# An uneven layout of w_down: 13 rows on the lower 64 partitions, 11 on the upper 64

## The chip, the cores and the metric

One core of one Trainium2 chip (trn2). The metric is the device time of one execution in microseconds; lower is better. "Span" is the time from the first to the last instruction in the profile, about 1.3 us less than the device time. In this document the lower engines are the DMA engines 0 to 7, and the upper ones 8 to 15.

## The reference, cut to what matters

One decode step of a transformer block, batch 2, width 640: a modulated layernorm, attention over a cache (32 heads, head size 192, the last 1024 positions), then a second modulated layernorm and a gated feed-forward layer with F = 1536.

```python
h = _layernorm(x) * (1 + ca) + sa
x = x + ga * _A_ref(h, A_k_cache, A_v_cache, A_wq, A_wo)
h = _layernorm(x) * (1 + cb) + sb
x = x + gb * (_gelu(h @ w_gate) * (h @ w_up) @ w_down)     # w_down: 1536 x 640, bf16
```

The kernel reads 76.88 MB, of which w_down is 1.97 MB. w_down is the last thing to be loaded.

## The kernel before

All large tensors are loaded by SyncE, in one fixed order, into one large SBUF tensor ("arena"), each load as soon as its space is free. Partition p of w_down holds rows 12p to 12p+11, so each partition has 12 rows of 1280 bytes. Four loads bring them: rows 9 to 11, 0 to 4, 5 to 7, 8.

```python
    WO_SPLIT = [(0, 28), (28, 17), (45, 3)]
    WD_SPLIT = [(9, 3), (0, 5), (5, 3), (8, 1)]
    ...
            if kind == "wd":
                r0, nr = WD_SPLIT[it[1]]
                return B_w_down.rearrange("(p r) n -> p (r n)", r=FC)[:, r0 * D:(r0 + nr) * D]
    ...
        def pump(*consumed):             # issues every load whose space is free
            ...
                queue["ops"][it] = S.dma("sp", k_dma(view(it), source(it)), sem_of[it], writes=keys(it), ...)
    ...
        # a = gelu(gate) * up, transposed to one column per row of w_down
        S.op("dve", lambda e: e.tensor_copy(out=aT[:, :, 0:RM:RB], in_=ps[:, 2, 0:FC * B]...), name="aT")
        for ci, (r0, nr) in enumerate(WD_SPLIT):
            def f(e, r0=r0, nr=nr):
                for fc in range(r0, r0 + nr):
                    wv = wd_v[:, fc, :].rearrange("p (i n) -> p i n", i=NR)
                    for i in range(NR):
                        last = e.matmul(ps[32 * i:32 * i + RM, BK_OT, CY:CY + DR], lhsT=aT[:, fc, :], rhs=wv[:, i, :], ...)
                return last
            S.op("pe", f, reads=["aT"] + keys(("wd", ci)), writes=[bank(BK_OT)], name="down%d" % ci)
        # then two VectorE operations (times gb, plus x) and the store
```

## Time and profile before

| | before |
|---|---|
| median, six runs | 186.31 us (186.21 to 186.68) |
| span of the profiled run | 185.0 us |
| DMA share of the chain that ended last | 57% |
| mean rate of the DMA engines | 416 GB/s |

The page's list of DMA queues. Its columns are packets, megabytes, and the time of those packets as a share of sixteen engines' span.

```profile
q1 hardware_dynamic: 3180, 76.88, 97.2%
q8 instruction: 5, 0.08, 0.2%
q10 hardware_dynamic: 16, 0.01, 0.0%
q14 instruction: 1, 0.01, 0.0%
```

The engines are busy with the kernel's own loads for 97% of the span.

The end of the chain of waits: start, duration, what.

```profile
155.23 26.50 DMA arena<-in_B_w_down_dram
181.73 0.04 issue
181.77 0.74 PE ps L690 x16
182.51 0.02 issue
182.54 0.34 DVE fin L695
182.87 0.02 issue
182.89 0.33 DVE finb L697
```

The down matmuls (L690) in the timeline: start, duration, engine, line, operation, operands, and in brackets how long the engine had been idle and what ended that.

```profile
179.88 0.39 PE L690 MATMUL ps<-arena,aT 128*17 128x160 bf16 x12 [0.30 <-DVE aT L682]
180.62 0.53 PE L690 MATMUL ps<-arena,aT 128*17 128x160 bf16 x20 [0.36 <-DMA arena<-in_B_w_down_dram]
181.77 0.71 PE L690 MATMUL ps<-arena,aT 128*17 128x160 bf16 x16 [0.62 <-DMA arena<-in_B_w_down_dram]
```

A load over 128 partitions is done when all sixteen engines have reported. The trace records each report. Here are two of the loads, their sixteen landings in order, in us from the start (worked out of the landing records, not a view of the profile):

```
first w_down load (rows 9-11): 176.66 .71 .75 .76 .80 .83 .96 177.08 .23 .39 .47 .77 | 178.33 .51 .60 .67
last w_down load (row 8):      180.23 .27 .28 .31 .38 .51 .62 .75 .94 .98 181.29 | 181.84 .90 182.03 .09 .12
```

All sixteen have the same bytes to move, yet four, and at the end five, are late. The five packets of the queue "instruction" start at 36.96, 96.64, 133.22, 160.87 and 178.05 us; each packet takes 0.99 to 1.08 us, and after each of them one more landing of every later load is late. (The 8 KB packet of queue 14, at 89.43 us, sets one engine back in the same way, by 1.0 us; that engine is not among the five, but is the next latest.) The Trainium skill, "Runtime: NRT & Kernel Launch", section "Instruction fetch mechanics", says that an engine's instruction memory is refilled in 16 KiB blocks, fetched by a DMA queue that the sequencer drives itself. The trace agrees: five packets of 16384 bytes, of the kind "instruction". The kernel's loads never pause, and no late engine caught up again before the end.

### The profile page before, as it was taken

The page shows a single profiled execution, that of the slowest core. Times are in us where ns is not written, and L with a number is a line of the kernel's source. Part 1 is how long each engine was busy: PE and PEld are TensorE (multiplying, and loading weights), DVE is VectorE, ACT ScalarE, POOL GpSimd, SP SyncE. Part 2 cuts the span into 40 slices and gives each one's busy share as a digit, 9 for nine tenths or more (in the row PEclk, how much of TensorE's full clock was granted, in tenths as well). Part 3 has the DMA queues.
Part 4 walks back from the last instruction along what each step waited for, and adds up shares of the span by engine and source line. Part 5 has one row for each costly group of instructions (what it writes and reads, how often), then busy time and mean ns, then how long its engine had stood idle before and what let it go on. Part 6 is the DMA issues. An engine that isn't in the chain of part 4 may idle for free.

```text
span 185.0 us, 1611 instructions
## 1 busy us (share of the span) xinstructions
PE 107.2 (58%) x835; PEld 28.5 (15%) x558; DVE 106.7 (58%) x99; ACT 14.5 (8%) x27; POOL 6.5 (4%) x27
## 2 busy tenths in 40 slices
PE   0015720857766379662499565966662499715472
PEld 0011100040000000001252000600001266401231
DVE  6213000119699488965991999789975938202411
ACT  2032100140000000001000000010001000101610
POOL 7600000000000000000000000000000000000000
PEclk9999995555799966998559999999999569996576
DMA  9989999999898989999998989899999999999990
GB/s 324 449 376 436 462 446 404 434 425 494 377 489 361 510 361 489 436 414 457 395 461 383 478 383 489 383 468 436 418 446 404 442 403 449 398 414 426 406 383 34
DMA packets 3202, 76.97 MB, mean 416 GB/s; under 512 B 378, under 2 KB 508, under 8 KB 1148
## 3 DMA queue, kind: packets, MB, share of 16 engines
q1 hardware_dynamic: 3180, 76.88, 97.2%
q8 instruction: 5, 0.08, 0.2%
q10 hardware_dynamic: 16, 0.01, 0.0%
q14 instruction: 1, 0.01, 0.0%
HBM read 76.88 MB, written 0.00 MB: 416 GB/s over the span
## 4 chain that ended last, share of the span: by engine, by line
DMA 57%; DVE 24%; PE 16%; ACT 1%; issue 1%; SPq 1%
DMA arena<-in_A_k_cache_dram 35%; DMA arena<-in_B_w_down_dram 14%; DVE arena L504 14%; PE ps L567 9%; DMA arena<-in_w_mod_dram 8%; DVE S_sb L523 6%; PE ps L516 3%; DVE Em L553 2%; PE ps L456 2%; DVE negm L533 1%; ACT E_sb L541 1%; SPq L283 1%; PE ps L544 1%; PE ps L537 1%; DVE M L529 0%
## 5 line engine op out<-in xcount | busy, mean ns | idle before, releaser
L516 PE MATMUL ps<-arena,ident_b 128*128 128x512 bf16 x192 | 51.3, 412 | 25.8 <-DVE arena L504 25.8
L504 DVE TENSOR_TENSOR arena<-arena,qbc 128x3072 bf16<-128x3072 bf16 x32 | 54.8, 1750 | 8.3 <-DMA arena<-in_A_k_cache_dram 8.3
L567 PE MATMUL ps<-arena,Em 128*64 128x384 bf16 x256 | 26.6, 379 | 5.7 <-DVE Em L553 5.7
L523 DVE TENSOR_REDUCE S_sb<-ps 128x32 f32<-128x1024 f32 x16 | 19.5, 1218 | 10.1 <-PE ps L516 10.1
L567 PEld LDWEIGHTS ps<-arena,Em 128*64 128x64 bf16 x256 | 16.4, 128 | 31.0 <-DVE Em L553 22.2
L553 DVE TENSOR_TENSOR Em<-E_sb,maskE 128x2048 bf16<-128x2048 bf16 x8 | 18.0, 2283 | 3.4 <-PE ps L567 3.4
L478 PE MATMUL ps<-arena,hT 128*2 128x512 bf16 x60 | 6.7, 625 | 9.1 <-DMA arena<-in_A_wq_dram 8.1
L531 PEld LDWEIGHTS ps<-ident_f,M 128*1 128x1 f32 x2 | 0.2, 80 | 60.5 <-DVE M L529 60.5
L488 DVE CAST qrow<-ps 128x512 bf16<-128x512 f32 x1 | 0.7, 692 | 15.0 <-PE ps L478 15.0
L627 PE MATMUL ps<-arena,oT 128*2 128x512 bf16 (+1 forms) x96 | 4.0, 312 | 4.7 <-DMA arena<-in_A_wo_dram 4.7
L635 DVE COPY arena<-ps 128x128 f32<-128x128 f32 x1 | 0.3, 292 | 10.5 <-PE ps L627 10.5
L541 ACT ACTIVATE E_sb<-S_sb,nbias 128x256 bf16<-128x256 f32 x2 | 1.0, 508 | 65.8 <-DVE nbias L539 65.8
L574 ACT ACTIVATE On<-ps,rden 128x384 bf16<-128x384 f32 x2 | 1.2, 580 | 49.5 <-PE ps L567 49.5
L397 PE MATMUL ps<-ident_b,crow 2*128 2x2 bf16 x5 | 0.4, 177 | 7.9 <-DMA crow<-in_c_dram 7.9
L456 PE MATMUL ps<-arena,scT 128*17 128x480 bf16 x40 | 4.3, 597 | 0.7 <-DMA arena<-in_w_mod_dram 0.7
L410 PE MATMUL ps<-st,selstat 128*128 128x2 f32 x4 | 1.1, 348 | 6.1 <-ACT sqj L406 6.1
L402 DVE CAST X<-xr 128x160 f32<-128x160 bf16 x1 | 0.2, 245 | 6.4 <-DMA xr<-in_A_x_dram 6.4
L661 PE MATMUL ps<-arena,h2T 128*2 128x384 bf16 x40 | 3.6, 507 | 0.3 <-DVE h2T L441 0.3
L494 PE MATMUL ps<-qrow,selq 128*128 128x192 bf16 x16 | 2.7, 361 | 1.2 <-ACT qrow L485 1.2
L464 DVE TENSOR_SCALAR opc<-modR 128x160 f32<-128x160 f32 x2 | 0.5, 244 | 4.7 <-ACT modR L461 4.7
L437 PE MATMUL ps<-selrow,hrow 128*32 128x2 bf16 x40 | 0.7, 182 | 3.6 <-DVE hrow L428 3.6
L478 PEld LDWEIGHTS ps<-arena,hT 128*2 128x2 bf16 x20 | 0.6, 107 | 14.3 <-DMA arena<-in_A_wq_dram 9.9
(84 smaller groups left out, 52.8 us busy)
## 6 DMA issues: line engine op xcount, KB each, us to landing
arena<-in_A_v_cache_dram SPq DMA_DIRECT2D x4, 6144.0 KB, 25.8
arena<-in_A_k_cache_dram SPq DMA_DIRECT2D x3, 6144.0 KB, 39.2
arena<-in_A_k_cache_dram SPq DMA_DIRECT2D x2, 3072.0 KB, 42.5
arena<-in_w_mod_dram SPq DMA_DIRECT2D x1, 4800.0 KB, 14.2
arena<-in_A_wq_dram SPq DMA_DIRECT2D x1, 4608.0 KB, 31.2
arena<-in_A_wo_dram SPq DMA_DIRECT2D x1, 4480.0 KB, 25.8
arena<-in_A_wq_dram SPq DMA_DIRECT2D x1, 3072.0 KB, 20.7
arena<-in_A_wo_dram SPq DMA_DIRECT2D x1, 2720.0 KB, 31.9
```

The costliest lines, as they stand in the source:

```text
L283: return lambda e: e.dma_start(dst, src)
L456: last = e.matmul(ps[32 * i:32 * i + RM, half, 0:MH].rearrange("p (m n) -> p m n", n=DR), lhsT=scT[:, k, :], rhs=wv[:, 3 * half:3 * half + ...
L478: last = e.matmul(ps[32 * i:32 * i + B, n, :], lhsT=hT[:, k, :], rhs=wv[:, kk, i, n * QW:(n + 1) * QW], start=(k == 0), stop=(k == KT - 1) ...
L494: last = e.matmul(ps[:, BK_T + b, 0:Dh], lhsT=selq[:, b, u * P:(u + 1) * P], rhs=qrow[:, u * Dh:(u + 1) * Dh], start=(u == 0), stop=(u == ...
L504: S.op("dve", lambda e: e.tensor_tensor(out=kt, in0=kt, in1=qbc[:, b, :].unsqueeze(1).broadcast_to([P, JC, Dh]), op=ALU.mult), reads=[("qb ...
L516: last = e.matmul(o_ap, lhsT=ident_b[:, :], rhs=kt[:, :, t * GC:(t + 1) * GC], start=(t == 0), stop=(t == NCH - 1))
L523: S.op("dve", lambda e: e.tensor_reduce(out=S_sb[:, b, 2 * JC * pair:2 * JC * (pair + 1)], in_=ps[:, 2 * z:2 * z + 2, :].rearrange("p k (j ...
L541: S.op("act", lambda e: e.activation(out=E_sb[:, b, :], in_=S_sb[:, b, :], func=ACTF.Exp, scale=SCALE, bias=nbias[:, b:b + 1], accum_out=d ...
L553: S.op("dve", lambda e, z=z, j=j: e.tensor_tensor(out=Em[:, z, :, :], in0=E_sb[:, b, j:j + JE].unsqueeze(2).broadcast_to([P, JE, H]), in1= ...
L567: last = e.matmul(ps[64 * i:64 * i + 2 * H, BK_O, 0:ON], lhsT=Em[:, z, 2 * jp:2 * jp + 2, :].rearrange("p j h -> p (j h)"), rhs=view(it, l ...
L627: last = e.matmul(ps[32 * i:32 * i + B, bk, 0:w], lhsT=oT[:, t, :], rhs=wv[:, tl, lo:lo + w], start=(t < NR), stop=(t >= NT - NR), tile_po ...
L661: last = e.matmul(ps[32 * i:32 * i + B, bk, 0:FT].rearrange("p (m r) -> p m r", r=FR), lhsT=h2T[:, k, :], rhs=wk[:, i, :, :], start=(k == ...
```

## The change

Its intent, as I read it: if the engines that end last are upper ones, let them carry less of the last tensor. Row 11 of each upper partition moves to the lower partition 64 below it. The Trainium skill, "DMA: Bandwidth & Descriptors", sections "The descriptor swizzle" and "Why a DMA increments its semaphore by 16 and not by 1", says that a load over 128 partitions gives partitions 0 to 63 to engines 0 to 7 and the others to 8 to 15, and that a load whose slowest dimension is 8 runs on the eight lowest engines only. So eight loads of eight partitions each bring both rows to the lower half. The upper half's two slots are zeroed by GpSimd, so whatever activations they meet have no effect; one more transpose matmul makes the thirteenth column of activations.

```diff
-    WD_SPLIT = [(9, 3), (0, 5), (5, 3), (8, 1)]
+    WD_SPLIT = [(9, 2), (FC - 1, 2), (0, 5), (5, 3), (8, 1)]
+    HALF = P // 2
+    XA, XB, XC = 8, 4, 2
...
+        def load_half(it):
+            z = view(it)
+            S.op("pool", lambda e: e.memset(z, 0.0), writes=keys(it), name="half0")
+            src = B_w_down.rearrange("(p r) n -> p r n", r=FC)[:, FC - 1, :].rearrange("(s c a b) n -> c b a s n", s=2, c=XC, a=XA)
+            for n in range(XB * XC):
+                c, b = divmod(n, XB)
+                p0 = c * XA * XB + b
+                S.dma("sp", k_dma(z[p0:(c + 1) * XA * XB:XB, :].rearrange("p (s n) -> p s n", s=2), src[c, b]), sem_of[it],
+                      writes=half_key(n) if n else keys(it), name="ld_half%d" % n)
...
+            c0 = 2 * FC
+            last = e.matmul(ps[0:HALF, 2, c0:c0 + B], lhsT=aR[:, :].rearrange("p (m r) -> p m r", r=FR)[:, HALF:P, FR - 1], rhs=selg[:, NR - 1, :],
+                            start=True, stop=True)
```

(Cut: the larger views, the thirteenth column of aT, and the keys that the down matmuls wait for.)

More of the change, by code (lines that the diff above doesn't have):

```diff
@@ L171, in bass_adaLN_cond__sliding_block_cached__geglu_ffn__decode_kernel @@
     WU_SPLIT = [(0, 3), (3, 2)]
-    WD_SPLIT = [(9, 3), (0, 5), (5, 3), (8, 1)]
+    WD_SPLIT = [(9, 2), (FC - 1, 2), (0, 5), (5, 3), (8, 1)]
+    HALF = P // 2
+    XA, XB, XC = 8, 4, 2
+    assert XA * XB * XC == HALF
     RB = 16
@@ L210, in bass_adaLN_cond__sliding_block_cached__geglu_ffn__decode_kernel @@
         for i, (r0, nr) in enumerate(WD_SPLIT):
-            place[("wd", i)] = (o_d + r0 * D, nr * D)
+            place[("wx" if r0 == FC - 1 else "wd", i)] = (o_d + r0 * D, nr * D)
         assert all(o % UNIT == 0 and n % UNIT == 0 and o + n <= NAR for o, n in place.values())
@@ L215, in bass_adaLN_cond__sliding_block_cached__geglu_ffn__decode_kernel @@
         wu_v = arena[:, o_u:o_u + KT * F].rearrange("p (k n) -> p k n", k=KT)
-        wd_v = arena[:, o_d:o_d + FC * D].rearrange("p (f n) -> p f n", f=FC)
+        wd_v = arena[:, o_d:o_d + (FC + 1) * D].rearrange("p (f n) -> p f n", f=FC + 1)
         qbc = sb("qbc", [P, B, Dh], BF16)
@@ L261, in bass_adaLN_cond__sliding_block_cached__geglu_ffn__decode_kernel @@
         selg = sb("selg", [P, NR, B], BF16)
-        aT = sb("aT", [P, FC, RM], BF16)
+        aT = sb("aT", [P, FC + 1, RM], BF16)
         fin = sb("fin", [P, DR], F32)
@@ L324, in source, with half_key @@
             return src[b][:, K0:Sk, :].rearrange("h (x j) d -> h x j d", x=XQ)[:, :, j0:j0 + n, :].rearrange("h x j d -> h x (j d)")
+        def half_key(n):
+            return [("half", n)] if n else []
+        def load_half(it):
[7 more added lines that the diff above has]
+                      writes=half_key(n) if n else keys(it), name="ld_half%d" % n)
         def pump(*consumed):
@@ L332, in pump @@
                     break
+                if it[0] == "wx":
+                    load_half(it)
+                    queue["next"] += 1
+                    continue
                 queue["ops"][it] = S.dma("sp", k_dma(view(it), source(it)), sem_of[it], writes=keys(it), name="ld_%s" % "_".join(str(z) for z in it))
@@ L679, in a_T @@
                                     start=True, stop=True)
+            c0 = 2 * FC
+            last = e.matmul(ps[0:HALF, 2, c0:c0 + B], lhsT=aR[:, :].rearrange("p (m r) -> p m r", r=FR)[:, HALF:P, FR - 1], rhs=selg[:, NR - 1, :],
+                            start=True, stop=True)
             return last
         S.op("pe", a_T, reads=["aR", "selg"], writes=[bank(2)], name="aT_T")
-        S.op("dve", lambda e: e.tensor_copy(out=aT[:, :, 0:RM:RB], in_=ps[:, 2, 0:FC * B].rearrange("p (f b) -> p f b", b=B)),
+        S.op("dve", lambda e: e.tensor_copy(out=aT[:, :, 0:RM:RB], in_=ps[:, 2, 0:(FC + 1) * B].rearrange("p (f b) -> p f b", b=B)),
              reads=[bank(2)], writes=["aT"], name="aT")
@@ L692, in f @@
                 return last
-            S.op("pe", f, reads=["aT"] + keys(("wd", ci)), writes=[bank(BK_OT)], name="down%d" % ci)
+            S.op("pe", f, reads=["aT"] + (keys(("wd", ci)) if r0 < FC - 1 else keys(("wx", ci)) + [z for n in range(XB * XC) for z in half_key(n)]), writes=[bank(BK_OT)], name="down%d" % ci)
         S.op("dve", lambda e: e.tensor_tensor(out=fin[:, :], in0=ps[:, BK_OT, CY:CY + DR], in1=modR[:, 5, :], op=ALU.mult),
```

## The prediction

> **What bounds the kernel.** Data movement. The page puts the DMA engines at 90% or more busy in nearly every slice, 416 GB/s over the span, and the chain of waits gives DMA 57%. It ends: w_down transfer until 181.73 us, 16 matmuls of L690 0.74 us, two vector operations, store; span 185.0 us. So only the last landing of w_down matters; PE work before it is covered.
>
> **Which engine is last.** The trace's landing records show sixteen completions per load. For the last w_down load (chunk of one row) eleven come at 180.23 to 181.29 us and five at 181.84 to 182.12. The five are late because of the queue "instruction": five packets of 16 KB, each about 1.0 us on one engine (at 37, 97, 133, 161, 178 us); after each of them one more landing of every following load is about 1.1 us late. This agrees with the Trainium skill, "Runtime: NRT & Kernel Launch", section "Instruction fetch mechanics" (refill in 16 KiB blocks by the sequencer's own DMA queue). So the lateness belongs to five particular engines, not to any amount of w_down.
>
> **What the change does.** By the Trainium skill, "DMA: Bandwidth & Descriptors", sections "Why a DMA increments its semaphore by 16 and not by 1" and "The descriptor swizzle", a 128-partition load gives partitions 0-63 to engines 0-7 and the others to 8-15, and an eight-row load uses only engines 0-7. Packet costs from the trace (start to next start): 1280 B 51 ns, 3840 B 145, 6400 B 240; so 2560 B about 98 (my estimate by interpolation). Upper engines: eight packets of 3840 B become 2560 B: -0.38 us. Lower engines: the same -0.38, plus sixteen packets of 1280 B (+0.82) and eight completions of about 10 ns (+0.08): +0.52 us. Total bytes are unchanged.
>
> Added off the path: seven or eight SyncE issues of 0.43 us (about 3.4 us, but issues run some 25 us ahead of landing); a GpSimd memset of 128x1280, about 1.1 us by scaling the 128x2112 one (1.86 us), on an idle engine at about 151-155 us; one more transpose matmul (0.04 us) and four more down matmuls (0.1 us) before the last wait.
>
> **Two cases.** The records don't name engines. The small c and x loads go, by their shape, to the lowest engines, and the packet sequences they sit in took none of the first fetches, as far as I can follow them.
> - All five late engines are upper ones (I give this about 65%; it must be the author's reason): the upper half lands at about 182.12-0.38 = 181.74, the lower at most 181.29+0.52 = 181.81. The end comes about 0.3 us earlier: 185.95.
> - At least one late engine is a lower one: its last landing moves to about 182.12+0.52 = 182.6; time about 186.75.
>
> Either way it is far under 2% (3.7 us). Point 186.1 us, range 185.6 to 186.9. Faster by over 2%: 1%; within 2%: 98%; slower by over 2%: 1%.
>
> **What the profile would show.** Queue q1: w_down packets of 2560 B on all engines, 128 more of 1280 B. Still five instruction fetches. The last load's landing times: the late group 0.38 us earlier, the early group partly 0.52 us later, so their gap closes; the last wait in the chain is still w_down, ended at 181.4 to 181.8. If instead some late landings go to 182.6, the late engines were in the lower half.
>
> **What would make it wrong.** The eight half loads cost more than their packets (a gap per load on the engines); the memset or the issues hold back SyncE so that the last loads start late; a sixth instruction fetch, or fetches that fall on other engines; the memset slows VectorE's work near 152 us by enough to reach the end, which I don't expect as the weights land later.

## More of the kernel before

TensorE was ready for the down matmuls at 179.88 us and was then held back twice by w_down. The work before them (second half of w_o, layernorm, gate, up, GELU) was ready about 1 us sooner than it had to be: the two waits for w_down are 0.36 and 0.62 us.

## The result, and the profile after

| | before | after |
|---|---|---|
| median, six runs | 186.31 us | 186.71 us |
| range | 186.21 to 186.68 | 185.91 to 186.90 |

The ratio of after to before is 1.0011 (95% interval 0.9991 to 1.0031). Ratios here are the mean time of one kernel's fast runs over that of the other's of the same rounds, so not quite the ratio of the medians that the table quotes. But look at the single runs: 185.91, 186.79, 186.35, 186.73, 186.70, 186.90. The new kernel is sometimes 0.4 us faster than before and mostly 0.4 us slower; the old one keeps within 0.5 us.

The trace of after is that of the 185.91 us execution. Its list of queues shows the added packets and, again, five instruction packets.

```profile
q1 hardware_dynamic: 3372, 76.88, 97.4%
q8 instruction: 5, 0.08, 0.2%
```

The end of its chain of waits (L681 is gate and up, L713 the down matmuls):

```profile
175.81 3.67 PE ps L681 x35
179.58 0.57 DVE aR L690
180.19 0.47 PE ps L698 x12
181.10 1.11 PE ps L713 x51
182.23 0.34 DVE fin L718
182.59 0.33 DVE finb L720
```

And the timeline's lines of the down matmuls and of the 40 w_o matmuls before them:

```profile
167.11 2.84 PE L647 MATMUL ps<-arena,oT 128*2 128x512 bf16 x40 [3.61 <-DMA arena<-in_A_wo_dram]
...
181.10 1.08 PE L713 MATMUL ps<-arena,aT 128*17 128x160 bf16 x52 [0.30 <-DVE aT L705]
```

No wait for w_down is left: all 52 down matmuls run in one go, as the last w_down landing came at 181.85 us (182.12 before). What ends last is the other chain, which begins when the 17-row w_o load lands at 167.1 us. The same 40 matmuls took 1.89 us before and 2.84 us here. Two lines of the table by stretches, the first of before and the second of after, show why. The columns after the stretch are busy times of PE, PEld, DVE, ACT and POOL, then the granted clock, the DMA share and GB/s.

```profile
167.00:170.00 3.00, 2.29 (x48) 0.72 (x28) 0.29 (x1) 0.60 (x1) 0.00 (x0) 0.68 1.05 445
```

```profile
167.00:170.00 3.00, 2.84 (x40) 0.66 (x20) 0.00 (x0) 0.00 (x0) 0.00 (x0) 0.50 1.03 438
```

The granted clock was 0.68 and 0.50 in this stage. So two questions: why are most executions slow, and is it the loads or this second chain?

### The profile page after: what moved, and what is told of

Same layout as the page of the kernel before. It is cut to its first block, busy times and chain, and to the rows that moved or that the text cites. A ratio compares the mean times of both kernels' runs of the same rounds, so it can differ in the third digit from the quotient of the medians.

```text
span 184.6 us, 1630 instructions
## 1 busy us (share of the span) xinstructions
PE 104.5 (57%) x840; PEld 28.1 (15%) x563; DVE 106.7 (58%) x99; ACT 14.5 (8%) x27; POOL 7.7 (4%) x28
## 4 chain that ended last, share of the span: by engine, by line
DMA 60%; DVE 21%; PE 16%; ACT 1%; issue 1%; SPq 0%; DVEq 0%
DMA arena<-in_A_k_cache_dram 35%; DMA arena<-in_A_wo_dram 17%; DVE arena L524 12%; DMA arena<-in_w_mod_dram 8%; DVE S_sb L543 4%; PE ps L587 4%; PE ps L536 3%; PE ps L476 2%; PE ps L681 2%; PE ps L647 2%; DVE Em L573 1%; PE ps L713 1%; DVE hrow L448 0%; PE ps L661 0%; PE ps L457 0%
## 5 line engine op out<-in xcount | busy, mean ns | idle before, releaser
L536 PE MATMUL ps<-arena,ident_b 128*128 128x512 bf16 x192 | 50.1, 405 | 29.9 <-DVE arena L524 29.8
L587 PE MATMUL ps<-arena,Em 128*64 128x384 bf16 x256 | 25.8, 370 | 5.6 <-DVE Em L573 5.6
L334 POOL MEMSET arena<- 128x1280 bf16 x1 | 1.2, 1165 | 146.4 <-PE ps L587 146.4
L647 PE MATMUL ps<-arena,oT 128*2 128x512 bf16 (+1 forms) x96 | 4.9, 369 | 4.0 <-DMA arena<-in_A_wo_dram 3.6
L681 PE MATMUL ps<-arena,h2T 128*2 128x384 bf16 x40 | 3.6, 508 | 0.3 <-DVE h2T L461 0.3
```

The lines of the kernel that those rows point to most:

```text
L334: S.op("pool", lambda e: e.memset(z, 0.0), writes=keys(it), name="half0")
L536: last = e.matmul(o_ap, lhsT=ident_b[:, :], rhs=kt[:, :, t * GC:(t + 1) * GC], start=(t == 0), stop=(t == NCH - 1))
L587: last = e.matmul(ps[64 * i:64 * i + 2 * H, BK_O, 0:ON], lhsT=Em[:, z, 2 * jp:2 * jp + 2, :].rearrange("p j h -> p (j h)"), rhs=view(it, l ...
L647: last = e.matmul(ps[32 * i:32 * i + B, bk, 0:w], lhsT=oT[:, t, :], rhs=wv[:, tl, lo:lo + w], start=(t < NR), stop=(t >= NT - NR), tile_po ...
L681: last = e.matmul(ps[32 * i:32 * i + B, bk, 0:FT].rearrange("p (m r) -> p m r", r=FR), lhsT=h2T[:, k, :], rhs=wk[:, i, :, :], start=(k == ...
```

## The experiments

Theory 1: w_down lands earlier now, but the second chain at a low clock hides it. Theory 2: the eight loads cost more than their packets in most executions. Theory 3, formed after the first batch: which engines take the instruction packets differs between executions, so the change helps or hurts by chance.

A tool that the changed kernel brings with it: its lower and upper engines have different amounts of work between the first and the last w_down load, so the landing records now tell the halves apart. By packet times (1280 B 51 ns, 3840 B 145, 6400 B 240, start to start) an upper engine needs 3.52 us and a lower one 4.42 us. The engine that takes the fifth instruction packet, which falls between the two loads, needs some 1.55 us more. When the sixteen landings of the two loads are paired by these sums, in each of six traces with the plain layout of the change (after, a_again, p1_after, p2_after, p3_after, f_after_wo) the four late engines, which are what I use below, fit one sum or the other within 0.1 us. The pairing is an inference, as no record names an engine; a check that does without it follows under p1_after.

### a_again: the changed kernel unaltered

No edit.

> The changed kernel unaltered, for a second trace and more times. Theory 1 (hidden by another chain): w_down now lands about 0.3 us earlier, but the work that starts at the last large w_o landing (about 167.0 us: 40 w_o matmuls, layernorm, gate and up, GELU, transpose) runs at a granted clock of 0.5 and reaches the down matmuls at 181.1 us or later, so they no longer wait for w_down; the time is 186.3 to 186.9 us and the trace shows no DMA wait before the last down matmuls. Theory 2 (the eight loads cost more than their packets in most executions): the last down matmuls wait for w_down and its last landing lies at 182.3 us or later.

Measured: 185.85, 186.94, 186.91, 187.04, 186.84, 186.16 us; ratio 1.0012 (0.9992 to 1.0031). The traced execution is again the fastest one: its last landing is at 181.82 us, and only the last four down matmuls wait shortly. Theory 1 fits this trace in the main (its 185.85 us lie below the 186.3 to 186.9 us that it expected), but a trace of a slow execution is what is wanted. The two-group pattern repeats.

### b_extra: the eight loads beside the full row

```diff
-    WD_SPLIT = [(9, 2), (FC - 1, 2), (0, 5), (5, 3), (8, 1)]
+    WD_SPLIT = [(9, 3), (FC, 2), (0, 5), (5, 3), (8, 1)]
```

(The two extra slots meet zero activations, so the result is right.)

> The eight loads are made beside the full row, so the lower engines get 0.9 us more than before and the upper ones nothing less; the result stays right (the extra rows meet zeros). If the five late engines are all upper ones: last landing of the lower ones 181.3 + 0.9 = 182.2 us, of the upper ones unchanged 182.1 us, so at most 0.1 to 0.3 us slower than before. If a late engine is a lower one: last landing 183.0 us and 0.7 us or more slower than before.

Measured: 186.96, 187.19, 187.16, 186.48, 186.81, 187.03 us, ratio 1.0028 (1.0015 to 1.0042). In its trace the last landing is at 182.94 us. Two engines that landed the first w_down load late, at 178.43 and 178.47 us, landed the last one 4.47 us later: they are lower ones. Two others, at 178.63 and 178.89 us, took 3.52 and 3.54 us: upper ones. So the late engines are not all of one half in this execution. That was the first sign of theory 3. The landing is where the second case had it (183.0 us); the median lies 0.6 us above that of before in the same rounds (186.39 us), a little under the 0.7 us expected.

### c_nohalf: without the eight loads

```diff
-            for n in range(XB * XC):
+            for n in range(0):
```

(And the waits for them. The result is wrong.)

> The changed kernel without its eight loads (result wrong on purpose: row 11 of each group of w_down is missing for all partitions). The last w_down landing comes at about 181.75 us on the late engines, lower engines about 0.9 us earlier than in the changed kernel. Theory 1: within 0.2 us of the changed kernel of the same rounds. Theory 2: faster than the changed kernel by 0.4 us or more.

Measured: 185.88, 185.98, 185.97, 185.82, 185.97 us; ratio 0.9974 (0.9962 to 0.9986). No slow group at all. The last landing is at 181.78 us against the expected 181.75. Compared with the fast executions of the changed kernel this is theory 1's outcome; with the slow ones it is theory 2's, which are 0.9 us slower. So the slow group is made by the eight loads and the rows that they carry, not by the clock. (This kernel also takes row 11 from all engines, so by itself it doesn't part the loads from the bytes.)

### d_nodown: no w_down load

```diff
+                if it[0] == "wd":
+                    queue["next"] += 1
+                    continue
```

(On top of c_nohalf; result wrong.)

> No w_down load at all (result wrong on purpose; down matmuls read stale values). This is the floor of the work after the w_o landing. Theory 1: only 0 to 0.6 us faster than the changed kernel, 185.7 to 186.5 us, though 1.6 MB of loads are gone. Theory 2: the w_down landing is what ends last, so 1.0 us or more faster than the changed kernel, at or below 185.2 us.

Measured: 185.21, 185.59, 185.63, 185.97, 185.66 us; ratio 0.9957 (0.9945 to 0.9970). With 2.0 MB less to load (the expectation's 1.6 MB was a slip) the kernel gains only 0.4%. The end of its chain:

```profile
175.07 3.67 PE ps L684 x35
178.84 0.57 DVE aR L693
179.46 0.47 PE ps L701 x12
180.36 1.11 PE ps L716 x52
181.49 0.34 DVE fin L721
```

This is the floor of the second chain: 185.2 to 186.0 us. Whatever is done to w_down alone, 0.8 us is about all there is to gain (186.4 minus 185.6, the medians of the same rounds). It was expected as 185.7 to 186.5; the floor is a little lower.

### p1_after, p2_after, p3_after: more traces of the changed kernel

No edit; other places in the order of runs, for other placements of the instruction packets.

> Changed kernel again, one execution with a trace. Theory 3, formed from the first batch: which engines take the five instruction fetches differs from execution to execution. If all the late engines are upper ones the last w_down landing is at about 181.85 us and the time 185.8 to 186.3 us; if a late engine is a lower one, its last landing lies 4.4 us behind its landing of the first w_down load instead of 3.5 us, at 182.4 to 182.7 us, and the time is 186.6 to 187.1 us. A slow time (186.6 or more) with the last landing below 182.0 us would refute it and speak for the granted clock instead.

> As p1_after, behind other kernels on the chip, for another placement of the fetches: either last landing near 181.85 us with 185.8 to 186.3 us, or last landing 182.4 to 182.7 us on a lower engine with 186.6 to 187.1 us.

> The changed kernel once more beside these two. Two groups again, 185.8 to 186.4 us and 186.6 to 187.1 us, with a mean 0.1 to 0.3% above before; g_onerow 0.3 to 0.5 us under its slow group, e_double about 0.5 us over it.

Measured: 186.88 us (p1_after), 186.78 us (p2_after), and 186.86, 186.66, 186.95, 186.45, 186.79 us (p3_after; ratio 1.0027, 1.0015 to 1.0039). All three traced executions are slow ones. p1_after's chain and down matmuls:

```profile
164.07 18.30 DMA arena<-in_B_w_down_dram
182.42 0.74 PE ps L713 x15
```

```profile
167.05 2.84 PE L647 MATMUL ps<-arena,oT 128*2 128x512 bf16 x40 [4.14 <-DMA arena<-in_A_wo_dram]
...
181.04 0.80 PE L713 MATMUL ps<-arena,aT 128*17 128x160 bf16 x36 [0.30 <-DVE aT L705]
182.42 0.71 PE L713 MATMUL ps<-arena,aT 128*17 128x160 bf16 x16 [0.58 <-DMA arena<-in_B_w_down_dram]
```

Everything up to the down matmuls is as in the fast execution: the same 2.84 us at L647, and the down matmuls begin at 181.04 us (181.10 there). The clock does not separate the two. What differs is the wait for w_down, which is back.

And here is why. The four latest landings of the first w_down load, and the same engines' landings of the last one, for the fast trace and the slow one (landing records, us):

```
after (185.91 us)      first      last    difference
                       177.97    181.48    3.51  upper
                       178.17    181.67    3.50  upper
                       178.24    181.73    3.48  upper
                       178.33    181.83    3.50  upper
p1_after (186.88 us)
                       178.07    181.60    3.53  upper
                       178.12    182.60    4.48  lower
                       178.16    181.70    3.54  upper
                       178.29    182.77    4.48  lower
```

In the fast execution all four engines that were already late are upper ones, and the change takes work from them. In the slow one two of them are lower ones, and the change gives them more. Both have five instruction packets. The other traces agree: a_again (185.85 us) has all four in the upper half; f_after_wo (186.75) has two of four in the lower half, p3_after (186.86) one, and p2_after (186.78) one or two, as there the engine of the fifth packet can be mistaken for a late one. One late lower engine is enough. Theory 3 holds in six traces out of six.

The check without pairing: only the engines that carry the eight small loads report their landings. The latest landing of the first w_down load is at 178.2 to 178.4 us in all six traces. The last of the 64 small landings is at 179.00 and 178.99 us in the two fast ones, and at 179.86 to 179.99 us in the four slow ones. So in the slow executions a latest engine had to carry the small loads as well, and in the fast ones none had. (In p2_after and f_after_wo the fifth packet comes at 178.0 and 178.1 us and could by itself have put off a small landing so far; for these two the pairing has to decide, and it fits within 0.1 us only with a late lower engine.)

Of p3_after's expectation, the 0.1 to 0.3% held and no run was as fast as 186.4 us. g_onerow's median came 0.3 us under p3_after's, as expected; e_double's came 0.2 us over it, with two runs more than 1 us over it, and not 0.5. The two groups are not quite clean: of the changed kernel's 19 runs three (186.16, 186.35 and 186.45 us) lie between them, and none of these was traced.

### f_after_wo and f_before_wo: the second chain shortened

```diff
-    WO_SPLIT = [(0, 28), (28, 17), (45, 3)]
+    WO_SPLIT = [(0, 28), (28, 9), (37, 8), (45, 3)]
```

(In both kernels; the new piece lies behind the one it was cut from.)

> Changed kernel with its 17-row w_o load cut into 9 and 8 rows, so that fewer w_o matmuls are left after the last big landing and the other chain ends 0.7 to 1.2 us earlier at a granted clock of 0.5. Theory 3: executions with late engines in the upper half alone become DMA-bound at a landing of about 181.85 us, 185.7 to 186.0 us; those with a late lower engine stay at 186.6 to 187.0 us, as w_down ends last there: the median hardly moves. If the other chain at low clock were what makes executions slow, the slow ones would disappear and all would be at 185.5 to 186.0 us.

> The kernel before with the same finer w_o load. Before waits for w_down whatever half the late engines are in, so the shorter other chain should change nothing: within 0.15 us of before (186.2 to 186.5 us), with no slow group. A gain of 0.3 us or more would show that the other chain, not w_down, bounded the kernel before in many executions.

Measured: f_after_wo 186.75, 187.05, 186.84, 186.19, 186.78, 186.70 us (ratio 1.0021, 1.0008 to 1.0033); f_before_wo 186.34, 186.58, 186.44, 186.58, 186.61 us (1.0010, 0.9998 to 1.0022). In f_after_wo's trace the down matmuls could begin at 180.17 us instead of 181.04, and still waited for w_down, until 181.09 and 182.28 us. So the slow group stays though the second chain ends earlier, as theory 3 has it. Before gains nothing, but this shows less than was meant: in f_before_wo's trace the down matmuls begin at 179.91 us, no sooner than in before (179.88), so its second chain was not shortened. f_before_wo was even 0.26 us slower by the medians, more than the 0.15 allowed, within an interval that includes no change. The fast executions of f_after_wo that I expected at 185.7 to 186.0 us didn't occur; the best was 186.19.

### g_onerow: eight loads with one row each

```diff
-                S.dma("sp", k_dma(z[p0:(c + 1) * XA * XB:XB, :].rearrange("p (s n) -> p s n", s=2), src[c, b]), ...
+                S.dma("sp", k_dma(z[p0:(c + 1) * XA * XB:XB, 0:D], src[c, b][:, 0, :]), ...
```

(The upper half's row 11 is missing; result wrong.)

> The changed kernel whose eight loads bring only the lower half's own row, not the upper half's (result wrong on purpose). Against before, upper engines -0.38 us, lower engines -0.38 + 8 x 0.051 + 8 x 0.010 = +0.11 us. Theory 3: executions with only upper engines late 185.9 us (the other chain's floor), those with a late lower one 186.4 us, none above 186.6 us. If instead the eight small loads themselves are what costs (a gap for each on the engines), the slow group stays at 186.7 to 187.0 us.

Measured: 186.53, 186.51, 186.37, 186.48, 186.92 us; ratio 1.0018 (1.0005 to 1.0031). Four of five lie 0.3 us below the slow group of the changed kernel (p3_after, same chip: median 186.79), the fifth above the bound of 186.6. That is between the two outcomes expected, and the landings say why. The mean of the sixteen landings moves on, from the first w_down load to the last, by the mean work of the sixteen engines, so no pairing is needed. (In each trace the fifth instruction packet falls between the two.) It moves by 3.62 us in before, 4.08 to 4.09 us in the six traces with the plain layout of the change, and 4.02 us here. All the surplus over before is the eight engines' with the small loads, so it counts double for each of them: 0.91 to 0.94 us with two rows in each small load, and 0.79 us with one. By packets and completions it should be 0.90 and 0.49 us. So half of the packets gave back only 0.1 to 0.15 us: the greater part of the cost goes with the number of loads, some 0.1 us each, and not with the rows that they carry. Theory 2 is right to that extent. But the cost is the same 0.91 to 0.94 us in the fast and the slow traces of the change, so it isn't what parts them; the placement is.

### e_double: two rows moved, sixteen loads

```diff
-    WD_SPLIT = [(9, 2), (FC - 1, 2), (0, 5), (5, 3), (8, 1)]
+    WD_SPLIT = [(9, 1), (FC - 2, 4), (0, 5), (5, 3), (8, 1)]
```

(With sixteen loads, a fourteenth slot, and one more transpose matmul; the result is right.)

> Twice the change: two rows of the upper half are moved, lower engines 14 rows in sixteen loads, upper 10 (result right). Against before, lower +1.04 us, upper -0.75 us. Theory 3: executions with a late lower engine end near 182.1 + 1.04 = 183.2 us, 187.3 to 187.5 us; those with late upper engines alone end with the slowest of the other lower engines, 182.3 us, about 186.5 us; most runs in the first group. If the change helped by evening out a fixed imbalance of the halves, the fast group would not move up by more than 0.2 us from the changed kernel's 185.9 us.

Measured: 186.87, 187.05, 186.73, 187.84, 186.71, 188.20 us; ratio 1.0054 (1.0030 to 1.0077). Even the fast group moved up, to 186.7 to 187.1 us, and the slow one to 187.8 and 188.2; both lie 0.2 to 0.9 us above what I expected, and fewer runs than expected were in the slow group. The traced execution (186.87 us) has its four late engines in the upper half, ending at 181.07 to 181.33 us, and yet the last landing is at 182.76 us, on lower engines that had not been late. So a fast placement no longer helps. By the mean of the landings (4.82 us from first to last) the sixteen loads cost each lower engine 2.40 us, against 1.80 by packets, which is 0.15 us a load. So the expectation undercounted the loads, as in g_onerow; what in a load takes the time I didn't find out.

c_nohalf, which takes one row from every engine, gains 0.4 us; to get that by relieving the late engines alone, a fixed layout would have to know them beforehand.

## Why the prediction was right or wrong

The measured 186.71 us lies in the stated range of 185.6 to 186.9, and "within 2%" was right. The range spans both of the prediction's cases (185.95 and 186.75 us), so that it was met says nothing about which case holds. Point by point:

- "Only the last landing of w_down matters": right for the kernel before, 181.77 us in the timeline. "PE work before it is covered" was true by about 1 us only. In the fast executions after the change it is not covered any more, and d_nodown puts its floor at 185.2 to 186.0 us.
- The costs by packets: right for the upper engines, 3.52 us from first to last load as summed (3.48 to 3.54 in the table above). For the lower ones the sum was right (4.48 us in the table, against 4.42) and its terms were not: with half the packets the eight loads still cost 0.79 us instead of 0.49 (g_onerow), and sixteen loads cost 2.40 us instead of 1.80 (e_double). "The eight half loads cost more than their packets", which the prediction lists under what would make it wrong, is so in part; that the sum came out for eight loads of two rows was luck.
- "About 1.1 us late" after each instruction packet: that is how far the latest landing stands behind the next latest after the first packet (40.81 us). The engine itself fell back by 1.55 to 1.71 us. The estimate doesn't rest on this figure.
- The two cases: both sizes were right. Case one, predicted 185.95, is seen at 185.85 and 185.91 us; case two, predicted 186.75, at 186.78 to 186.88 us.
- The step that failed: "All five late engines are upper ones (I give this about 65%; it must be the author's reason)". I took the placement for a property of the kernel, to be guessed once. The traces show that it is not: two traced executions of the unaltered changed kernel had the late engines in the upper half only, three had one or two of four in the lower half. Of its 19 runs 14 took 186.66 us or more. By the untraced runs' times alone, case two is the common one. So my point of 186.1, which leaned to the rarer case, was 0.6 us low.
- The last wait "ended at 181.4 to 181.8": in the fast trace there was no such wait, as the second chain was later; in the slow one it ended at 182.37.
- SyncE's issues: predicted 0.43 us each, measured 0.67 to 0.84 us for most of the eight loads. They still cost nothing, as the last w_down load was issued at 164.3 us and landed 17.6 us later. The memset took 1.17 us (1.1 predicted), beside VectorE's work, without effect.

What stays open: what decides which engines take the instruction packets in an execution, and in which half they fell in the trace of before, as that kernel's landings don't tell the halves apart. That the slow untraced executions have the same cause as the traced ones is inferred from their times. The traces whose placements differ were also taken on different chips (a_again on chip 1, p1_after and p2_after on 15, p3_after on 6; the chip of after is not on record). That the placement differs between executions on one chip rests on the times alone: a_again's six runs go from 185.85 to 187.04 us. And why an eight-row load costs its engines some 0.1 us whatever it carries was not tested.

## What to carry to other kernels

When a kernel keeps all DMA engines busy to the end, look at the spread of the last load's sixteen landings, and at what other queues take from single engines, before moving bytes between engines. A static shift of work pays only for a lateness that sits on the same engines in every execution; so trace several executions, above all those of the common time, not only the first. Measure the floor without the suspected load first: here it limited the gain to 0.4%. And when a sum of costs comes out right, change one of its terms alone before believing the others: g_onerow did so, and most of the cost turned out to sit in the number of loads.

## What the Trainium skill lacked or had wrong

- "Runtime: NRT & Kernel Launch", section "Instruction fetch mechanics", calls the cost of crossing a 16 KiB boundary "mostly hidden". Where loads never pause it isn't hidden from them: each refill's packet took about 1.0 us, and left the landings of one DMA engine 1.55 to 1.71 us late for the rest of the execution (trace of before).
- No page that I read says which DMA engine serves a refill. Here it differed between traced executions of one kernel: late engines in the upper half only (185.85 and 185.91 us) or in both halves (186.78 to 186.88 us).
- "DMA: Bandwidth & Descriptors", section "Rules for kernel authors", says of transfers under 64 KB that one pays mostly overhead, but not how much of a DMA engine's time in a backlogged queue. The runs point the same way and give a number: eight loads of 20 KB cost each of their engines 0.91 to 0.94 us, and eight of half that size still 0.79 us.
- The same page gives no issue times by a load's shape. In the trace of after, SyncE took 0.67 to 0.84 us for most loads of eight partitions with two rows each, and 0.43 us for the w_down load of 128 partitions issued just before them.
